# Mish as one ScalarE function, and the layer norm's root by Newton steps on VectorE

## The chip, the cores and the metric

The kernel runs on one core of a Trainium2 chip. Its time is the device time of one execution in microseconds; the time before is the median of three runs. The engines are called as the profile calls them: PE is TensorE (matmuls), ACT is ScalarE, DVE is VectorE, POOL is GpSimd, and SP issues the DMAs.

## What is computed

The reference normalizes `x` (2048 rows of 512) and adds three things: `x` itself, a spectral filter of the normalized rows, and an MLP of them with the Mish activation. Everything is float32.

```python
xn = (x - mean) / sqrt(var + 1e-5)                     # x: (1, 2048, 512)
A  = irfft2(rfft2(xn) * (w_r + 1j * w_i))              # w_r, w_i: (2048, 257)
h  = xn @ w1 + b1                                      # w1: (512, 1792)
sp = log1p(exp(-abs(h))) + where(h > 0, h, 0)          # softplus
B  = (h * tanh(sp)) @ w2                               # w2: (1792, 512)
out = x + A + B
```

## The kernel before

**Precision.** Every float32 operand of a matmul is split into a high and a low float16 part, and each product is three matmuls (`mm3`, lines 64, 67 and 68: high by high, high by low, low by high). A split (`split`, lines 200 and 201) is one pass of ScalarE, which scales and writes the high part, and one of VectorE, which writes the remainder. Before a split, operands are scaled by powers of two that the kernel derives on the chip: of w1 from sums of squares (`load_w1`, `pow2_norm`), of w2 and of the spectral weights from maxima (`w2_scale`, `prep_spectral`). The last step of each is a reduction over the partitions on GpSimd (`qs`, `qa`, and `am` at line 308).

**The MLP.** The 2048 rows are four groups `g` of 512, and the 1792 hidden columns are 14 tiles `f` of 128, so there are 56 tiles. For each tile, `mlp_up` makes `ph` (128 hidden columns by 512 rows) in PSUM by 12 matmuls of 512 columns. Then come six passes for the activation (lines 535 to 543) and the split into `a` (two float16 parts). `mlp_down` makes 12 matmuls that add the tile to four accumulators `pa` in PSUM. It follows `mlp_up` by `LAG` = 2 tiles. `ph` has two PSUM buffers (pool `ps_h`, shared with the transposes `pt`), `hb` and `a` have three each. When a group is done, `mlp_end` adds `x` and writes `m` (line 572), which frees the accumulators.

The activation works on `hb`, which is `h` in units of a power of two. It uses tanh(softplus(h)) = 1 - 2/(n + 2) with n + 2 = (e + 1)^2 + 1 and e = exp(h): a capped copy (VectorE, line 537), exp, square, ln and exp (ScalarE, lines 538 to 542), and the product (VectorE, line 543). The sign is undone by the scale of the split, `s_act`.

**The norm.** `norm(g, ...)` takes statistics of four slices of 128 rows (lines 120 and 122), then the reciprocal root of the variance `ve` for all four at once: ln and exp on ScalarE (lines 126 and 128) and one Newton step on VectorE (lines 131 to 135). `rs` is the result times 1024. Each slice is then normalized (`xs`, line 144), split (`xh`, line 152 on ScalarE, line 153 on GpSimd, in group 0 on VectorE), transposed on TensorE (`pt`, line 157), and copied to `xnT` (lines 158 and 159).

**The transform.** The 2048 by 512 transform is a series of small matmuls: `psS` (first step, `s1_forward`), then for each of four chunks `c` the units `psP`, the spectrum (`ere`, `eim`, `ore`, `oim`, with products on VectorE and GpSimd and the split `u`), `psA`, `psT`, and last `psY` (`s1_inverse`). Between the steps the data goes through DRAM (`d_y1`, `d_a`, `d_t`).

**The order.** All loads are issued by SP. The body is written as one sequence in which the MLP's half tiles are placed between the other work: `b(n)` issues `n` tiles, and `stream_a` is interleaved by counts (`B_END`, `N_UNITS`). The framework then orders each engine's instructions itself, by its own estimate of when they can start; `issue_after` and `keep_in_program_order` tie a few of them. On the chip each engine works through its list strictly in order, so an instruction that waits holds up all that stand behind it.

Of the kernel before, what the change touches and what calls it, by code (L numbers as in the profile page):

```python
# [11 lines left out]
F16 = mybir.dt.float16  # L12
F32 = mybir.dt.float32
# [6 lines left out]
P = 128  # L20
# [9 lines left out]
# column offsets of the packed small constants (fp16 columns)  # L30
# [5 lines left out]
def spectral_mlp_kernel(ctx, tc, x, wt, w0, w1, b1, w2, cT, cIT, cM, out):  # L36
# [14 lines left out]
    nc.scalar.preload_act_table_set("natural_log_exp_and_others")  # L51
# [3 lines left out]
    half = cp.tile([P, 1], F32, tag="half", name="half")  # L55
    nc.gpsimd.memset(half, 0.5)

    d_y1 = dp.tile([64, P, 256], F16, tag="d_y1", name="d_y1")  # [(s2 d2)][(c f1)][hl d1]
    d_a = dp.tile([16, P, 4 * 256], F16, tag="d_a", name="d_a")  # [f1g][(k2p cc j)][f1l hl d1]
    d_t = dp.tile([64, P, 256], F16, tag="d_t", name="d_t")  # [(s2 d2)][(c f1)][hl d1]  # L60

    def mm3(ps, stat, mov, start, stop, order=False):
        """stat(h), mov(h): operands by part; ps += hi*hi + hi*lo + lo*hi"""
        first = nc.tensor.matmul(ps, stat(0), mov(0), start=start, stop=False)  # L64
# [3 lines left out]
        nc.tensor.matmul(ps, stat(1), mov(0), start=False, stop=stop)  # L68

# [45 lines left out]

    def norm(g, ts):
# [8 lines left out]
        lv = sp.tile([P, 4], F32, tag="lv", name=f"lv_{g}", bufs=2)  # L125
        nc.scalar.activation(lv, ve, AF.Ln)
        rr = sp.tile([P, 4], F32, tag="rr", name=f"rr_{g}", bufs=2)
        nc.scalar.activation(rr, lv, AF.Exp, scale=-0.5)
        # a newton step: r <- r * (1.5 - 0.5 v r^2), the result times 2^10
        q1 = sp.tile([P, 4], F32, tag="q1", name=f"q1_{g}", bufs=2)  # L130
        nc.vector.tensor_mul(q1, rr, rr)
        nc.vector.tensor_mul(q1, q1, ve)
# [32 lines left out]
    def pow2_of(name, am, n=1, out_tag=None):  # L165
        """largest powers of two at or below am (at least 2^-60)"""
# [14 lines left out]
    def pow2_norm(name, q, n):  # L181
        """q: n sums of squares per partition; power of two p with sqrt(the whole sum) < 2p"""
# [7 lines left out]
        # halve the exponent: the bits are multiples of 2^23  # L190
# [26 lines left out]
    def load_w1(k):  # L217
        """part k of w1: loaded, and its scale"""
# [21 lines left out]
        # h of these columns comes in units of 2^24/p1  # L240
        s_b = scalars(f"b_{k}", w1sc[k], 1024.0)
        f2 = slice(2 * a, 2 * b)
        nc.vector.tensor_scalar(bs[:, f2], b1t[:, f2], s_b, None, op0=ALU.mult)
        s_cap[k] = scalars(f"cap_{k}", s_b, 9.5)
# [7 lines left out]
    def act_scale():  # L252
        # |h| <= |xn| |w1 column| + |b1| with |xn| < 23
# [5 lines left out]
        s_a = scalars("a", pH, 2.0**14, recip=True)  # L259
        for k in range(2):  # L260
            t = cp.tile([P, 1], F32, tag=f"s_act{k}", name=f"s_act_{k}")
            nc.vector.scalar_tensor_tensor(t, s_a, -1.0, s_exp[k], op0=ALU.mult, op1=ALU.mult)
            s_act[k] = t
# [28 lines left out]
    def prep_spectral():  # L292
# [6 lines left out]
        # chunk c at partitions 32c + f1g: [+re,-re,+im,-im][r][j f1l]  # L299
# [12 lines left out]
        # coefficient tables of slot 0: A' = c0 A + c1 B, B' = c2 A + c3 B  # L312
# [47 lines left out]
    def spectrum(c):  # L360
# [50 lines left out]
        X = tp.tile([P, 4, 256], F32, tag="X", name=f"X_{c}", bufs=2)  # pr, mr, pi, mi  # L411
# [29 lines left out]
        if c == 0:  # L441
            # f = 0 (A) and f = 1024 (B): real sequences with their own weights
# [49 lines left out]
            # partitions (cc j f1l)  # L492
# [27 lines left out]
    macc, yacc = {}, {}  # L520

    def mlp_up(g, f):
        """a tile of hidden columns, and its activation split in two parts"""
# [11 lines left out]
        nc.scalar.activation(hb, ph, AF.Identity, bias=bs[:, f : f + 1])  # L535
        e = mp.tile([P, 512], F32, tag="e", name=f"e_{g}_{f}", bufs=3)
        nc.vector.tensor_scalar(e, hb, s_cap[k], None, op0=ALU.min)  # L537
        nc.scalar.activation(e, e, AF.Exp, scale=s_exp[k])  # L538
        # tanh(softplus(h)) = 1 - 2/(n + 2) with n = e^2 + 2e = (e + 1)^2 - 1
        nc.scalar.activation(e, e, AF.Square, bias=1.0)  # L540
        nc.scalar.activation(e, e, AF.Ln, scale=0.5, bias=half)  # L541
        nc.scalar.activation(e, e, AF.Exp, scale=-1.0)  # L542
        nc.vector.scalar_tensor_tensor(hb, e, 1.0, hb, op0=ALU.subtract, op1=ALU.mult)  # L543
        a = mp.tile([P, 2, 512], F16, tag="a", name=f"a_{g}_{f}", bufs=3)
        split(a[:, 0, :], a[:, 1, :], hb, s_act[k])
# [16 lines left out]
    def mlp_end(g):  # L562
        # the group's transposed rows are done with: x + MLP takes their place
# [12 lines left out]
    def mlp_all():  # L576
        """the MLP, half a tile of hidden columns at a time"""
# [51 lines left out]
    def b(n):  # L629
        """n tiles up, and those down that go with them"""  # L630
# [5 lines left out]
    def stream_a():  # L636
        todo = []  # P2' units, each some way behind its D' unit
# [75 lines left out]
    # the last step of the transform: the last group before its MLP ends, the others as fillers  # L713
# [175 lines left out]
```

## Time and profile before

| | |
|---|---|
| device time, median of 3 runs | 440.85 us (438.7 to 442.54) |
| span of the profiled execution, first to last instruction | 440.4 us |
| difference between the median and that span | 0.45 us |
| TensorE busy | 395.2 us (90%), 2099 matmuls |
| ScalarE busy | 308.5 us (70%), 493 instructions |
| VectorE busy | 301.3 us (68%), 545 instructions |
| GpSimd busy | 44.1 us (10%), 46 instructions |
| share of the 16 DMA engines' span in use by the main queue | 43.2% |
| mean granted TensorE clock | 0.982 of full speed |

The profile is of one execution, whose own device time is not listed apart from the runs; its span is the nearest measure of it. Busy matmuls are pipelined, so a matmul counts for longer than the distance to the next one. In a list of waits, "A <- B" means that engine and line A was idle until B was done. A row of the timeline has the start, the duration, the engine, the line, what is written and read, and in brackets how long the engine was idle just before and what ended that.

### The profile page before, as it was taken

The numbers are of one execution on the slowest core, as the hardware profiler recorded it, in microseconds if no ns is written. First come the engines' busy times: TensorE is split into PE (matmuls) and PEld (weight loads), VectorE is DVE, ScalarE is ACT, GpSimd is POOL, SyncE is SP. The second block draws the span as 40 slices with busy tenths as digits, with TensorE's granted clock in tenths as the row PEclk, the third lists the DMA queues.
The fourth block names the chain that finished last, engine by engine and source line by source line (L and its number), as shares of the span: only waits on it lengthen the run. The fifth ranks groups of instructions, "written<-read, shape, count | busy, mean of one in ns | idle before, by whom it ended". The sixth has DMA issues, their size and how long they took to land. (4 is left out here: it accounts for less than half of the span.)

```text
span 440.4 us, 5858 instructions
## 1 busy us (share of the span) xinstructions
PE 395.2 (90%) x2099; PEld 193.2 (44%) x2099; DVE 301.3 (68%) x545; ACT 308.5 (70%) x493; POOL 44.1 (10%) x46
## 2 busy tenths in 40 slices
PE   0785899699797999989999999999989998899995
PEld 0332344344343445435554445544455544454442
DVE  4969999888557335895569875578855598444564
ACT  2999998867768778468764868756786657576640
POOL 0000003232040000220002020020200022000000
PEclk9998999899899999999999999999999999899999
DMA  8998754487232721032246013342024210233786
GB/s 245 282 360 287 246 188 138 127 262 262 91 101 90 212 80 49 1 89 71 81 142 216 25 48 115 103 133 83 2 71 148 93 50 0 70 122 104 224 292 239
DMA packets 48813, 61.04 MB, mean 139 GB/s; under 512 B 3168, under 2 KB 31360, under 8 KB 48528
## 3 DMA queue, kind: packets, MB, share of 16 engines
q1 hardware_dynamic: 48784, 60.67, 43.2%
q8 instruction: 16, 0.26, 0.2%
q14 instruction: 13, 0.11, 0.1%
HBM read 43.85 MB, written 16.78 MB: 138 GB/s over the span
## 5 line engine op out<-in xcount | busy, mean ns | idle before, releaser
L64 PE MATMUL ph<-xnT,w1t 128*128 128x512 f16 x224 | 85.4, 381 | 5.4 <-ACT hb L535 4.4
L68 PE MATMUL ph<-xnT,w1t 128*128 128x512 f16 x224 | 85.4, 382 | 3.6 <-DVE w1t L201 3.6
L64 PE MATMUL pa<-w2t,a 128*128 128x512 f16 x224 | 85.3, 383 | 2.4 <-DVE m L572 2.4
L68 PE MATMUL pa<-w2t,a 128*128 128x512 f16 x224 | 86.2, 385 | 0.0
L67 PE MATMUL pa<-w2t,a 128*128 128x512 f16 x224 | 86.0, 384 | 0.0
L67 PE MATMUL ph<-xnT,w1t 128*128 128x512 f16 x224 | 85.4, 381 | 0.0
L543 DVE SCALAR_TENSOR_TENSOR hb<-e,hb 128x512 f32<-128x512 f32 x56 | 42.5, 759 | 56.0 <-ACT e L542 55.4
L200 ACT ACTIVATE a<-hb,s_act 128x512 f16<-128x512 f32 x56 | 40.3, 720 | 28.7 <-DVE hb L543 28.7
L538 ACT ACTIVATE e<-e,sc_exp 128x512 f32<-128x512 f32 x56 | 40.2, 719 | 28.1 <-DVE e L537 27.9
L535 ACT ACTIVATE hb<-ph,bs 128x512 f32<-128x512 f32 x56 | 37.9, 677 | 27.4 <-PE ph L68 27.0
L201 DVE SCALAR_TENSOR_TENSOR a<-hb,s_act,a 128x512 f16<-128x512 f32 x56 | 45.6, 813 | 16.6 <-ACT a L200 16.5
L541 ACT ACTIVATE e<-e,half 128x512 f32<-128x512 f32 x56 | 40.4, 721 | 1.6
L537 DVE TENSOR_SCALAR e<-hb,sc_cap 128x512 f32<-128x512 f32 x56 | 28.0, 500 | 16.2 <-ACT hb L535 16.1
L542 ACT ACTIVATE e<-e 128x512 f32<-128x512 f32 x56 | 35.2, 628 | 1.4
L540 ACT ACTIVATE e<-e 128x512 f32<-128x512 f32 x56 | 35.1, 627 | 1.2
L68 PEld LDWEIGHTS <-w1t 128*128 128x128 f16 x224 | 22.0, 98 | 31.1 <-DVE w1t L201 4.5
L67 PEld LDWEIGHTS <-w1t 128*128 128x128 f16 x224 | 22.0, 98 | 30.5 <-issue 6.3
L67 PEld LDWEIGHTS <-a 128*128 128x128 f16 x224 | 22.2, 99 | 27.2 <-issue 4.0
L68 PEld LDWEIGHTS <-a 128*128 128x128 f16 x224 | 22.1, 99 | 26.9 <-issue 1.0
L64 PEld LDWEIGHTS <-w1t 128*128 128x128 f16 x224 | 22.0, 98 | 26.7 <-ACT w1t L200 1.6
L64 PEld LDWEIGHTS <-a 128*128 128x128 f16 x224 | 22.1, 99 | 24.3 <-issue 0.9
L157 PE MATMUL pt<-cMt,xh 128*128 128x128 f16 x128 | 11.6, 244 | 18.7 <-ACT xh L152 11.5
(162 smaller groups left out, 608.5 us busy)
## 6 DMA issues: line engine op xcount, KB each, us to landing
x<-in_x_dram SPq DMA_DIRECT2D x8, 512.0 KB
d_y<-y SPq DMA_DIRECT2D x8, 512.0 KB
wm<-in_wt_dram SPq DMA_DIRECT2D x8, 512.0 KB
yt<-d_y SPq DMA_DIRECT2D x16, 256.0 KB
d_a<-at SPq DMA_DIRECT2D x16, 256.0 KB
ai<-d_a SPq DMA_DIRECT2D x16, 256.0 KB
d_t<-tt SPq DMA_DIRECT2D x16, 256.0 KB
yi<-d_t SPq DMA_DIRECT2D x16, 256.0 KB
```

Of the source, the lines that this page charges most:

```text
L64: first = nc.tensor.matmul(ps, stat(0), mov(0), start=start, stop=False)
L67: nc.tensor.matmul(ps, stat(0), mov(1), start=False, stop=False)
L68: nc.tensor.matmul(ps, stat(1), mov(0), start=False, stop=stop)
L200: hi = nc.scalar.activation(dst_h, src, AF.Copy, scale=scale)
L201: nc.vector.scalar_tensor_tensor(dst_l, src, scale, dst_h, op0=ALU.mult, op1=ALU.subtract)
L535: nc.scalar.activation(hb, ph, AF.Identity, bias=bs[:, f : f + 1])
L537: nc.vector.tensor_scalar(e, hb, s_cap[k], None, op0=ALU.min)
L538: nc.scalar.activation(e, e, AF.Exp, scale=s_exp[k])
L540: nc.scalar.activation(e, e, AF.Square, bias=1.0)
L541: nc.scalar.activation(e, e, AF.Ln, scale=0.5, bias=half)
L542: nc.scalar.activation(e, e, AF.Exp, scale=-1.0)
L543: nc.vector.scalar_tensor_tensor(hb, e, 1.0, hb, op0=ALU.subtract, op1=ALU.mult)
```

## The change

**The activation.** `mlp_up` now has one ScalarE pass, the function Mish, which reads `ph` from PSUM, multiplies by `s_exp` (so that `h` comes in its own units) and adds the bias `b1`. The tiles `e`, the caps `s_cap`, the scaled bias `bs`, the constant `half` and the negative scales `s_act` are gone. The split into `a` stays, with the scale `sc["a"]`. Of the six passes for each tile one is left: ScalarE has two passes for each tile in place of six (with the split), and VectorE one in place of three.

**The root.** `rsqrt_of` takes a first value from the bits of `ve` by one integer operation, and makes three Newton steps of three VectorE instructions each; the last instruction multiplies by -128, which makes up for the constants left out of the steps. That is eleven instructions on VectorE in place of two on ScalarE and four on VectorE, each on 128 by 4 values.

**The table.** The function table that ScalarE loads at the start is now the one with Mish, in place of the one with ln and exp. The program has one table load, as before.

```diff
-    nc.scalar.preload_act_table_set("natural_log_exp_and_others")
+    nc.scalar.preload_act_table_set("mish")
...
+    def rsqrt_of(g, ve):
+        r = sp.tile([P, 4], F32, tag="rr", name=f"rr_{g}_0", bufs=4)
+        nc.vector.tensor_scalar(
+            r.bitcast(I32), ve.bitcast(I32), -0.5, float(0x5F3759DF), op0=ALU.mult, op1=ALU.add
+        )
+        for k in range(3):
+            t = sp.tile([P, 4], F32, tag="rt", name=f"rt_{g}_{k}", bufs=2)
+            nc.vector.tensor_mul(t, r, r)
+            q = sp.tile([P, 4], F32, tag="rq", name=f"rq_{g}_{k}", bufs=2)
+            nc.vector.scalar_tensor_tensor(q, t, 0.25**k, ve, op0=ALU.mult, op1=ALU.mult)
+            n = sp.tile([P, 4], F32, tag="rr", name=f"rr_{g}_{k + 1}", bufs=4)
+            nc.vector.scalar_tensor_tensor(n, q, 3.0, r, op0=ALU.subtract, op1=ALU.mult)
+            r = n
+        rs = sp.tile([P, 4], F32, tag="rs", name=f"rs_{g}", bufs=2)
+        nc.vector.tensor_scalar(rs, r, -128.0, None, op0=ALU.mult)
+        return rs
...
-        nc.scalar.activation(lv, ve, AF.Ln)
-        nc.scalar.activation(rr, lv, AF.Exp, scale=-0.5)
-        nc.vector.tensor_mul(q1, rr, rr)
-        nc.vector.tensor_mul(q1, q1, ve)
-        nc.vector.tensor_scalar(q1, q1, -512.0, 1536.0, op0=ALU.mult, op1=ALU.add)
-        nc.vector.tensor_mul(rs, rr, q1)
+        rs = rsqrt_of(g, ve)
...
-        nc.scalar.activation(hb, ph, AF.Identity, bias=bs[:, f : f + 1])
-        nc.vector.tensor_scalar(e, hb, s_cap[k], None, op0=ALU.min)
-        nc.scalar.activation(e, e, AF.Exp, scale=s_exp[k])
-        nc.scalar.activation(e, e, AF.Square, bias=1.0)
-        nc.scalar.activation(e, e, AF.Ln, scale=0.5, bias=half)
-        nc.scalar.activation(e, e, AF.Exp, scale=-1.0)
-        nc.vector.scalar_tensor_tensor(hb, e, 1.0, hb, op0=ALU.subtract, op1=ALU.mult)
+        nc.scalar.activation(hb, ph, AF.Mish, bias=b1t[:, f : f + 1], scale=s_exp[k])
         a = mp.tile([P, 2, 512], F16, tag="a", name=f"a_{g}_{f}", bufs=3)
-        split(a[:, 0, :], a[:, 1, :], hb, s_act[k])
+        split(a[:, 0, :], a[:, 1, :], hb, sc["a"])
```

With other instructions in the program the framework's order changes too. Three places matter below. Lines of the new kernel are some 10 lower than those of the old for the same statement.

**TensorE, the first product with w2.** In the names, `ph_0_6` is group 0, tile 6, and `pa_0_0` is the first of group 0's four accumulators. Before:

```order
L64 MATMUL ph_0_6_559<-xnT_0_124,w1t_92 128x512
L64 LDWEIGHTS a_0_0_294
L64 MATMUL pa_0_0_416<-w2t_93,a_0_0_294 128x512
L64 LDWEIGHTS a_0_0_294
L64 MATMUL pa_0_1_417<-w2t_93,a_0_0_294 128x512
```

Now:

```order
L64 MATMUL ph_0_7_551<-xnT_0_133,w1t_90 128x512
L65 LDWEIGHTS w1t_90
L65 MATMUL ph_0_7_551<-xnT_0_133,w1t_90 128x512
L61 LDWEIGHTS a_0_0_282
L61 MATMUL pa_0_0_390<-w2t_91,a_0_0_282 128x512
```

Before, seven of the twelve matmuls of tile 6 stood ahead of the first `pa`; now all of tiles 6 and 7 do, 17 matmuls more. Behind this point the order of TensorE's work is nearly the same in both.

**VectorE, the root of norm 1.** `xs_4` is the first normalized slice of group 1, `st_2` and `st_3` are statistics of groups 2 and 3, and `a_0_7` is a split. Before:

```order
L131 TENSOR_TENSOR q1_1_736<-rr_1_734 128x4
L120 BN_STATS st_2_997<-x_2_0_992 128x6
L201 SCALAR_TENSOR_TENSOR a_0_6_581<-hb_0_6_572,s_act_1_270,a_0_6_581 128x512
L132 TENSOR_TENSOR q1_1_736<-q1_1_736,ve_1_730 128x4
L120 BN_STATS st_2_997<-x_2_0_992 128x6
L133 TENSOR_SCALAR q1_1_736<-q1_1_736 128x4
L120 BN_STATS st_2_997<-x_2_1_994 128x6
L135 TENSOR_TENSOR rs_1_740<-rr_1_734,q1_1_736 128x4
L120 BN_STATS st_2_997<-x_2_1_994 128x6
L543 SCALAR_TENSOR_TENSOR hb_0_7_618<-e_0_7_620,hb_0_7_618 128x512
L144 TENSOR_SCALAR xs_4_743<-x_1_0_600,mv_1_721,rs_1_740 128x512
```

Now (the chain has begun 12 rows ahead of these):

```order
L139 BN_AGGR mv_2_907<-st_2_906 128x2 x2
L127 SCALAR_TENSOR_TENSOR rr_1_2_669<-rq_1_1_667,rr_1_1_663 128x4
L137 BN_STATS st_3_1145<-x_3_0_1140 128x6
L123 TENSOR_TENSOR rt_1_2_671<-rr_1_2_669 128x4
L141 TENSOR_SCALAR ve_2_916<-mv_2_907 128x4
L137 BN_STATS st_3_1145<-x_3_0_1140 128x6
L125 SCALAR_TENSOR_TENSOR rq_1_2_673<-rt_1_2_671,ve_1_655 128x4
L127 SCALAR_TENSOR_TENSOR rr_1_3_675<-rq_1_2_673,rr_1_2_669 128x4
L117 TENSOR_SCALAR rr_2_0_918<-ve_2_916 128x4
L130 TENSOR_SCALAR rs_1_677<-rr_1_3_675 128x4
L123 TENSOR_TENSOR rt_2_0_920<-rr_2_0_918 128x4
L151 TENSOR_SCALAR xs_4_680<-x_1_0_546,mv_1_646,rs_1_677 128x512
```

The longer chain has more statistics between its steps, those of `x_3_0` among them, which is loaded after `x_2`.

**VectorE, the scale of the spectral weights.** `cl_W` reads `am`, GpSimd's reduction; `xnT_2` are the copies that free the buffers of group 2's transposes, and `y1_8` frees a buffer of the first transform step. Before:

```order
L158 COPY xnT_2_1019<-pt_8_1025 128x4x128
L543 SCALAR_TENSOR_TENSOR hb_0_13_967<-e_0_13_969,hb_0_13_967 128x512
L158 COPY xnT_2_1019<-pt_9_1048 128x4x128
L106 SCALAR_TENSOR_TENSOR y1_8_1040<-psS1_8_1036,y1_8_1040 128x4x128
L201 SCALAR_TENSOR_TENSOR a_0_13_976<-hb_0_13_967,s_act_1_270,a_0_13_976 128x512
L158 COPY xnT_2_1019<-pt_10_1071 128x4x128
L106 SCALAR_TENSOR_TENSOR y1_8_1040<-psS1_9_1059,y1_8_1040 128x4x128
L158 COPY xnT_2_1019<-pt_11_1094 128x4x128
L168 TENSOR_SCALAR cl_W_1546<-am_1544 128x1
```

Now:

```order
L208 SCALAR_TENSOR_TENSOR a_0_13_885<-hb_0_13_883,sc_a_264,a_0_13_885 128x512
L175 TENSOR_SCALAR cl_W_1430<-am_1428 128x1
L177 TENSOR_SCALAR p2_W_1432<-cl_W_1430 128x1
L165 COPY xnT_2_940<-pt_8_946 128x4x128
L183 RECIPROCAL sc_u_1434<-p2_W_1432 128x1
L185 TENSOR_SCALAR sc_k_1437<-p2_W_1432 128x1
L185 TENSOR_SCALAR sc_u_1434<-sc_u_1434 128x1
L165 COPY xnT_2_940<-pt_9_969 128x4x128
```

The wait for `am` stood behind all four copies of group 2 and now stands ahead of the first.

More of the change, by code (lines that the diff above doesn't have):

```diff
@@ L49, in spectral_mlp_kernel @@
     dp = ctx.enter_context(tc.tile_pool(name="dp", bufs=1, space=bass.MemoryType.DRAM))
-    nc.scalar.preload_act_table_set("natural_log_exp_and_others")
+    nc.scalar.preload_act_table_set("mish")
     xv = x.rearrange("(p s) d -> p s d", s=NS2)
     outv = out.rearrange("(p s) d -> p s d", s=NS2)
-    half = cp.tile([P, 1], F32, tag="half", name="half")
-    nc.gpsimd.memset(half, 0.5)
     d_y1 = dp.tile([64, P, 256], F16, tag="d_y1", name="d_y1")
@@ L124, in norm @@
         nc.vector.tensor_scalar(ve, mv[:, :, 1], 1e-5, None, op0=ALU.add)
-        lv = sp.tile([P, 4], F32, tag="lv", name=f"lv_{g}", bufs=2)
-        nc.scalar.activation(lv, ve, AF.Ln)
[L127 to L132, printed above, removed]
-        nc.vector.tensor_scalar(q1, q1, -512.0, 1536.0, op0=ALU.mult, op1=ALU.add)
-        rs = sp.tile([P, 4], F32, tag="rs", name=f"rs_{g}", bufs=2)
-        nc.vector.tensor_mul(rs, rr, q1)
+        rs = rsqrt_of(g, ve)
         xT = cp.tile([P, 2, 4, 512], F16, tag=f"xnT{g}", name=f"xnT_{g}")
@@ L207, in spectral_mlp_kernel @@
     b1t = cp.tile([P, NFC], F32, tag="b1", name="b1t")
-    bs = cp.tile([P, NFC], F32, tag="bs", name="bs")
-    s_cap, s_exp, s_act = {}, {}, {}
+    s_exp = {}
     sc = {}
@@ L239, in load_w1 @@
         w1sc[k] = scalars(f"w1_{k}", p1, 2.0**14, recip=True)
[L241 to L244, printed above, removed]
         s_exp[k] = scalars(f"exp_{k}", p1, 2.0**-24)
@@ L258, in act_scale @@
         pH = pow2_of("H", hb_)
[L259 to L263, printed above, removed]
+        sc["a"] = scalars("a", pH, 2.0**14, recip=True)
         sc["pH"] = pH
@@ L534, in mlp_up @@
         hb = mp.tile([P, 512], F32, tag="hb", name=f"hb_{g}_{f}", bufs=3)
[L535 to L543, printed above, removed]
+        nc.scalar.activation(hb, ph, AF.Mish, bias=b1t[:, f : f + 1], scale=s_exp[k])
         a = mp.tile([P, 2, 512], F16, tag="a", name=f"a_{g}_{f}", bufs=3)
-        split(a[:, 0, :], a[:, 1, :], hb, s_act[k])
+        split(a[:, 0, :], a[:, 1, :], hb, sc["a"])
         return a
```

## Prediction

> **What bounds the kernel now.** I read the page first for the engine that is fullest, then the busy time by stage, then the waits of that engine.
>
> ```profile
> PE 395.2 (90%) x2099; PEld 193.2 (44%) x2099; DVE 301.3 (68%) x545; ACT 308.5 (70%) x493; POOL 44.1 (10%) x46
> PE   0785899699797999989999999999989998899995
> PEclk9998999899899999999999999999999999899999
> ```
>
> TensorE (PE) is busy for 395.2 of 440.4 us. ScalarE (ACT) and VectorE (DVE), from which the change takes work, are busy for only 70 and 68%. So removed work does not count by its own length; it counts where TensorE waits for it, at most 440.4 - 395.2 = 45.2 us and what a lowered clock costs. The next view has the engines' busy time by stage (columns: stretch, length, then busy us and count for each engine, granted clock, DMA share, GB/s).
>
> ```profile
> 0.00:48.00 48.00, 26.69 (x126) 11.82 (x127) 35.78 (x90) 37.73 (x61) 2.25 (x9) 0.96 0.89 289
> 48.00:76.00 28.00, 28.00 (x131) 12.73 (x130) 27.35 (x51) 25.36 (x40) 2.81 (x2) 1.00 0.59 191
> 76.00:141.00 65.00, 55.08 (x306) 26.93 (x304) 48.40 (x91) 48.88 (x86) 15.60 (x19) 0.95 0.49 155
> 141.00:381.00 240.00, 231.33 (x1282) 116.58 (x1279) 159.28 (x271) 168.13 (x267) 23.42 (x16) 0.99 0.27 85
> 381.00:441.00 60.00, 54.09 (x264) 25.14 (x261) 30.50 (x46) 28.35 (x44) 0.00 (x0) 0.98 0.58 189
> ```
>
> TensorE's idle time is 21.3 us in the first stage (loading, first norm, w1 and w2 scales), 0 in the second, 9.9 in the third (norms 1 to 3 between MLP tiles), 8.7 in the fourth (transform and MLP together) and 5.9 at the end. The second stage gives the price of a large matmul that waits for nothing: 28.00 / 131 = 0.214 us. The granted clock is a loss that is no idle time. The page's clock line has an 8 in four of its slices of 11 us (the 4th, 8th, 11th and 35th); the stage means say what one costs: 0.95 over 65 us is 3.3 us lost for two of them, 0.96 over 48 us 1.9 for one. I use 1.7 for each. Whom TensorE waited for (us in total, times, longest):
>
> ```profile
> PE pt L157 <- ACT xh L152: 11.5, 1, 11.5
> PE pt L157 <- ACT xnT L159: 7.1, 3, 3.6
> PE ph L64 <- ACT hb L535: 4.4, 3, 1.7
> PE ph L68 <- DVE w1t L201: 3.6, 2, 3.3
> PE psA L64 <- ACT u L200: 3.1, 4, 1.6
> PE pa L64 <- DVE m L572: 2.4, 3, 1.3
> PE oim L64 <- DVE w L452: 2.1, 1, 2.1
> PE psA L68 <- DVE u L201: 1.9, 4, 0.7
> ```
>
> None of these is the wait for an activated tile `a`: the activation itself is hidden by the two tiles of lag. All are waits for other work in the queues of ScalarE and VectorE, behind which the six passes stand.
>
> **The activation, by its price.** The removed and kept passes, from the page (count | busy, mean ns of one):
>
> ```profile
> L543 DVE SCALAR_TENSOR_TENSOR hb<-e,hb 128x512 f32<-128x512 f32 x56 | 42.5, 759 | 56.0 <-ACT e L542 55.4
> L538 ACT ACTIVATE e<-e,sc_exp 128x512 f32<-128x512 f32 x56 | 40.2, 719 | 28.1 <-DVE e L537 27.9
> L535 ACT ACTIVATE hb<-ph,bs 128x512 f32<-128x512 f32 x56 | 37.9, 677 | 27.4 <-PE ph L68 27.0
> L541 ACT ACTIVATE e<-e,half 128x512 f32<-128x512 f32 x56 | 40.4, 721 | 1.6
> L537 DVE TENSOR_SCALAR e<-hb,sc_cap 128x512 f32<-128x512 f32 x56 | 28.0, 500 | 16.2 <-ACT hb L535 16.1
> L542 ACT ACTIVATE e<-e 128x512 f32<-128x512 f32 x56 | 35.2, 628 | 1.4
> L540 ACT ACTIVATE e<-e 128x512 f32<-128x512 f32 x56 | 35.1, 627 | 1.2
> ```
>
> ScalarE loses 40.2 + 35.1 + 40.4 + 35.2 = 150.9 us and falls to about 158; VectorE loses 42.5 + 28.0 = 70.5. The new pass takes the place of L535 with one more per-partition operand. The trace has no Mish, so I bound it: 0.677 us (L535, also from PSUM) below, and above 2.7 us, as if it cost the four removed passes together. I take 0.72, the row with a scale operand; either end keeps ScalarE below TensorE's 5.1 us for a tile (24 x 0.214), so the ends change the sum by no more than the range below.
>
> **The root, by its price.** Rows of the first norm: two steps of the old chain, the first pass on VectorE that uses it, and ScalarE's square of w1 ahead of the cast that the transposes wait for.
>
> ```profile
> 8.18 0.16 DVE L131 TENSOR_TENSOR q<-rr 128x4 f32<-128x4 f32 x1 [0.51 <-ACT rr L128]
> 8.38 0.16 DVE L132 TENSOR_TENSOR q<-q,ve 128x4 f32<-128x4 f32 x1
> 8.98 1.00 DVE L144 TENSOR_SCALAR xs<-x,mv,rs 128x512 f32<-128x512 f32 x2
> 9.76 1.06 ACT L230 ACTIVATE w1t<-w1s 128x1024 f16<-128x1024 f32 x1 [1.61 <-DMA w1s<-in_w_dram]
> ```
>
> A dependent step is 0.20 us. Eleven steps after 7.68 (end of `ve`) end near 9.9, so `xs` starts about 0.9 later than 8.98. The cast stands behind the square, which ends at 10.82 because its DMA came late; `xs` is there by 10.4. I cost this at nothing; without that cover it would be 0.9 us. In the later norms the steps are interleaved: before the first `xs` of norm 1 the new queue has the statistics of x_3_0, a load later than in the old one, and norm 2's first steps. GpSimd, which makes the low parts, sets the pace of those norms anyway.
>
> **First stage: 3 us gained.** TensorE now does 17 more `ph` matmuls before the first `pa`: 17 x 0.214 = 3.6 us of work done while it waits for w2's scale. That scale does not come sooner: three w1 splits that stood behind it on VectorE now stand ahead, and take the time that the cap and product passes leave. The longest hole stays, as the four w2 reductions still precede the w1 split:
>
> ```profile
> 35.94 0.61 PE L68 MATMUL ph<-xnT,w1t 128*128 128x512 f16 x1 [3.27 <-DVE w1t L201]
> ```
>
> So 3.0, with bounds of 0 (the scale is late by what was won) and 6 (two of the three `hb` waits go too).
>
> **Third stage: 6.6 us gained.** The two long waits of the transposes, and what surrounds them:
>
> ```profile
> 80.71 1.21 DVE L297 TENSOR_REDUCE mxw<-wm 128x1 f32<-128x1024 f32 x1
> 82.53 0.57 ACT L159 COPY xnT<-pt 128x512 f16<-128x512 f16 x1
> 83.14 0.92 PE L157 MATMUL pt<-cMt,xh 128*128 128x128 f16 x8 [3.58 <-ACT xnT L159]
> 112.85 0.61 PE L157 MATMUL pt<-cMt,xh 128*128 128x128 f16 x8 [2.78 <-ACT xnT L159]
> 116.03 0.38 POOL L308 PARTITION_ALL_REDUCE am<-mxwa  x1 [9.28 <-DVE y L106]
> 124.23 2.26 POOL L153 TENSOR_TENSOR xh<-xs,xh 128x512 f16<-128x512 f32 x2 [7.82 <-ACT e L541]
> ```
>
> The first wait (3.58) I keep whole: ScalarE's copy comes sooner, but VectorE's copy still stands behind the wm reduction and now behind norm 2's and 3's steps. The second (2.78) loses ScalarE's four passes, but in the new VectorE queue the scale that needs `am` moves ahead of the first transposed copy. GpSimd idles 9.28 us before that all-reduce and 7.82 after it, beside an extra unnamed row of its own in the program, and I take both to stay. The reductions ahead of it come some 9 us sooner, since their queue waits less for ScalarE, so I put `am` at about 107 (116.4 before) and TensorE there at 106: 1.0 of the wait is left, 1.8 goes, and the slow clock behind it, 1.7. The `m` waits (2.4) and the last transposes' 0.7 (7.1 - 3.6 - 2.8) go with the passes among them. 1.8 + 1.7 + 2.4 + 0.7 = 6.6; bounds -5 (`am` no sooner than before: TensorE would wait 10.4 there in place of 2.8, less the other 3.1) and 13 (9.9 + 3.3).
>
> That clock is the place for one rule: the waits of 3.58 and 2.78 end in the 8th and 11th slice, which show the lower clock, and the 2.1 of `oim`, near 191 us in the 18th, shows none. [...]
>
> **Fourth stage: 7.5 us gained.** Behind `oim` stands a serial chain of VectorE, GpSimd, ScalarE, VectorE to `psA`:
>
> ```profile
> 369.78 0.68 DVE L469 TENSOR_TENSOR o<-oim,wO 128x512 f32<-128x512 f32 x1
> 370.60 1.76 DVE L543 SCALAR_TENSOR_TENSOR hb<-e,hb 128x512 f32<-128x512 f32 x1
> 372.28 0.68 DVE L470 TENSOR_TENSOR o<-oim,wO 128x512 f32<-128x512 f32 x1
> ```
>
> The removed L543 sits inside it for 1.76 us, with others ahead. Of the 5.0 us of `psA` waits I leave 1.0, of 2.1 for `oim` 1.0 (it also moves up by 8 matmuls on TensorE), and take 0.7 from the 1.6 that are left of the stage's 8.7: 4.0 + 1.1 + 0.7, and 1.7 of slow clock in the 35th slice, just behind the chain shown. Bounds 3 (one long `psA` wait and its clock) and 10.4 (8.7 + 1.7).
>
> **The end: 0.5.** TensorE's last matmul is the bound there:
>
> ```profile
> 435.52 0.38 PE L68 MATMUL pa<-w2t,a 128*128 128x512 f16 x1
> ```
>
> The chain of waits runs through the last tile's six passes, but TensorE has inverse-transform and `pa` work under them until 435.5. What follows stays.
>
> **The sum.** 3.0 + 6.6 + 7.5 + 0.5 = 17.6: 440.4 - 17.6 = 422.8 for a profiled span. The median of the runs, 440.85, lies 0.45 above the span: **423 us**.
>
> **Rivals.**
> *Nearly all waits go.* TensorE keeps only the start and the tail: the sum by the upper bounds is 6 + 13 + 10.4 + 1 = 30.4, so 410. For it: ScalarE at 158 us has room everywhere. Against it: VectorE's queue is in order and full of waits for loads. Chance 0.15 (under 415).
> *The holes stay where loads and GpSimd make them.* Stage three gives 0 and stage one 1: 440.85 - 9 = 432, or 436 with half of stage four. For it: the 9.28 and 7.82 us of GpSimd, and the DMA share of 0.89 in the first stage. Chance 0.19.
> *Slower, by `am`.* The place is VectorE's queue at the second transposes, now closed until `am` comes. Each us that `am` is later than 107 costs one, and a long wait costs 1.7 of clock: from 107 + 17.6 - 1.7 = 123 on the kernel is slower than before, and at 130 it takes 448. The longer root chain and the statistics ahead of it can delay `am`; against it stands that before, with all passes in the queue, it came at 116.4. Chance 0.04.
> *The one function isn't one.* If Mish shared no table with copy and square, each tile would switch tables twice:
>
> ```profile
> 0.72 1.28 ACT L51 ACT_TABLE_LOAD   x1 [0.72 <-PEq L862]
> ```
>
> 112 x 1.28 = 143 us would give back what ScalarE won (150.9), and the time would be about 440. Against it: the new program has one table load, as the old. Chance 0.02. [...]
>
> **How the numbers follow.** The forecast (415 to 431) has the remaining 0.60. A change within 1% can't be told from none here; 1% of 440.85 puts the limits at 436.4 and 445.3. The table case and 0.03 of the second rival fall between, 0.03 of the third above: 0.92, 0.05, 0.03. The range runs from the first rival's 410 to 434, inside the second's.
>
> **What would show it.** Right: ScalarE near 158 busy, VectorE near 235, one Mish row of 0.68 to 0.75 us; waits of `psA` under 1.5 in sum; the first `pa` still near 47, with 8 `ph` tiles done; a wait of `pt` near 80 still there, with a slow clock behind it. Wrong: `am` after 112, a wait of TensorE for `a`, or the first `pa` after 50.

## The result, and the profile after

The changed kernel takes **425.75 us** (median of 4 runs, 424.21 to 427.87); the kernel before took 440.12 beside it (median of 4, 438.70 to 442.54). The ratio is 0.969 with a 95% interval of 0.964 to 0.975. The profiled execution has a span of 424.4 us. In a later series of runs the same program gave 424.39 (0.968, 0.964 to 0.971). The forecast was 423, with 410 to 434 as its range.

The page of the changed kernel, busy time and the two lines that were shown of before:

```profile
PE 391.0 (92%) x2099; PEld 194.1 (46%) x2099; DVE 241.3 (57%) x453; ACT 172.4 (41%) x261; POOL 42.2 (10%) x45
PE   0787899499899999989999999999999999999995
PEclk9999999889999999989999999999999999999999
```

ScalarE gave up 136 us of busy time and VectorE 60; the kernel got 16 us shorter in its span. TensorE is busy 4.2 us less and idle 11.8 us less (33.4 for 45.2). Where the idle time went is read from the stages (columns as before: stretch, length, busy us and count of PE, PEld, DVE, ACT, POOL, granted clock, DMA share, GB/s; the last stretch reaches past the span by 0.6):

```profile
0.00:48.00 48.00, 29.32 (x142) 13.72 (x143) 34.95 (x83) 30.24 (x45) 2.75 (x8) 1.00 0.90 294
48.00:76.00 28.00, 27.24 (x136) 12.52 (x134) 26.69 (x61) 15.40 (x21) 4.39 (x4) 1.00 0.60 187
76.00:141.00 65.00, 57.99 (x317) 28.49 (x314) 41.73 (x77) 29.13 (x49) 13.27 (x18) 0.95 0.57 178
141.00:381.00 240.00, 237.87 (x1334) 122.27 (x1333) 119.81 (x208) 90.43 (x138) 21.75 (x16) 0.99 0.27 86
381.00:425.00 44.00, 38.59 (x178) 17.10 (x176) 18.12 (x26) 7.20 (x10) 0.00 (x0) 0.98 0.66 215
```

TensorE's idle time by stage is now 18.7, 0.8, 7.0, 2.1 and 4.8 us (21.3, 0, 9.9, 8.7 and 5.3 before, the last one without the 0.6 us past the span). The fourth stage gave most. The third gave 2.9 us of idle time and nothing of slow clock, where 6.6 us were foretold with both. Whom TensorE waits for (us in total, times, longest):

```profile
PE pt L164 <- ACT xh L159: 11.3, 1, 11.3
PE pt L164 <- ACT xnT L166: 6.6, 2, 5.6
PE ph L65 <- DVE w1t L208: 2.4, 2, 2.1
PE oim L61 <- DVE w L450: 2.1, 1, 2.1
PE pa L61 <- ACT w2t L207: 1.6, 1, 1.6
```

`psA` and `m` have left the list, and no row names `a`. One wait has grown: the transposes' 3.6 us near 80 us is now 5.6. The new pass, by the page:

```profile
L533 ACT ACTIVATE hb<-ph,b1t,sc_exp 128x512 f32<-128x512 f32 x56 | 43.4, 775 | 107.4 <-PE ph L65 104.2
```

Mish costs 0.775 us for 128x512 from PSUM. ScalarE now stands idle for 107.4 us ahead of it, nearly all of that for the matmul that feeds it.

### The profile page after: what moved, and what is told of

It reads as the page before. It is cut to its first block, busy times and chain, and to the rows that moved or that the text cites. A ratio compares the mean times of both kernels' runs of the same rounds, so it can differ in the third digit from the quotient of the medians.

```text
span 424.4 us, 5542 instructions
## 1 busy us (share of the span) xinstructions
PE 391.0 (92%) x2099; PEld 194.1 (46%) x2099; DVE 241.3 (57%) x453; ACT 172.4 (41%) x261; POOL 42.2 (10%) x45
## 4 chain that ended last, share of the span: by engine, by line
PE 72%; DVE 13%; DMA 6%; ACT 4%; issue 2%; POOL 0%; SPq 0%; DVEq 0%; ACTq 0%; POOLq 0%
PE pa L65 9%; PE pa L64 9%; PE pa L61 9%; PE ph L61 9%; PE ph L65 9%; PE ph L64 9%; DVE q L273 2%; DMA w1s<-in_w_dram 2%; PE pt L164 2%; ACT w1t L236 1%; PE psA L61 1%; PE psA L64 1%; PE psA L65 1%; DMA w2s<-in_w_dram 1%; DMA ai<-d_a 1%
## 5 line engine op out<-in xcount | busy, mean ns | idle before, releaser
L533 ACT ACTIVATE hb<-ph,b1t,sc_exp 128x512 f32<-128x512 f32 x56 | 43.4, 775 | 107.4 <-PE ph L65 104.2
L208 DVE SCALAR_TENSOR_TENSOR a<-hb,sc_a,a 128x512 f16<-128x512 f32 x56 | 42.3, 755 | 76.2 <-ACT a L207 76.1
L207 ACT ACTIVATE a<-hb,sc_a 128x512 f16<-128x512 f32 x56 | 40.1, 719 | 2.2 <-PE pa L65 0.9
L65 PEld LDWEIGHTS <-w1t 128*128 128x128 f16 x224 | 21.9, 98 | 29.7 <-DVE w1t L208 3.4
L64 PEld LDWEIGHTS <-w1t 128*128 128x128 f16 x224 | 21.9, 98 | 27.1 <-issue 2.3
L61 PEld LDWEIGHTS <-w1t 128*128 128x128 f16 x224 | 21.9, 98 | 26.4 <-ACT w1t L207 1.6
L164 PE MATMUL pt<-cMt,xh 128*128 128x128 f16 x128 | 12.3, 253 | 18.5 <-ACT xh L159 11.3
L487 DVE SCALAR_TENSOR_TENSOR at<-psA,at 128x512 f16<-128x512 f32 x16 | 11.0, 689 | 19.1 <-ACT at L486 19.1
L422 POOL TENSOR_TENSOR w<-X,wE 128x512 f32<-128x512 f32 x4 | 5.1, 1269 | 165.7 <-ACT er L387 76.8
L164 PEld LDWEIGHTS <-xh 128*128 128x128 f16 x128 | 10.3, 114 | 23.7 <-ACT xh L159 12.0
L509 DVE SCALAR_TENSOR_TENSOR tt<-psT,tt 128x512 f16<-128x512 f32 x16 | 11.0, 690 | 14.1 <-ACT tt L508 13.9
L160 POOL TENSOR_TENSOR xh<-xs,xh 128x512 f16<-128x512 f32 x12 | 14.4, 1216 | 45.2 <-ACT xh L159 29.9
L486 ACT ACTIVATE at<-psA 128x512 f16<-128x512 f32 x16 | 9.4, 589 | 22.8 <-PE psA L65 22.8
```

Of the source, the lines that this page charges most:

```text
L160: (nc.vector if g == 0 else nc.gpsimd).tensor_sub(xh[:, 1, :], xs, xh[:, 0, :])
L164: nc.tensor.transpose(pt[:, h, dc, :], xh[:, h, dc * P : (dc + 1) * P], ident)
L207: hi = nc.scalar.activation(dst_h, src, AF.Copy, scale=scale)
L208: nc.vector.scalar_tensor_tensor(dst_l, src, scale, dst_h, op0=ALU.mult, op1=ALU.subtract)
L486: nc.scalar.mul(at[:, :, 0, :], ps, 2.0**-15)
L487: nc.vector.scalar_tensor_tensor(at[:, :, 1, :], ps, 2.0**-15, at[:, :, 0, :], op0=ALU.mult, op1=ALU.subtract)
```

## The experiments

All times are medians beside runs of the kernel before on the same chip; the ratio is to those runs. The rows come from several series on different chips, and the kernel before had medians from 439.02 to 441.03 in them; so two rows are compared by their ratios too, and 2 us between two medians show nothing by themselves. "Idle" is TensorE's, from the same five stretches of each profile (length less busy time; the last one up to the span's end).

| kernel | us | ratio, 95% interval | idle 0-48 | 48-76 | 76-141 | 141-381 | rest | clock |
|---|---|---|---|---|---|---|---|---|
| before | 440.12 | 1 | 21.3 | 0 | 9.9 | 8.7 | 5.3 | 0.982 |
| changed | 425.75 | 0.969 (0.964-0.975) | 18.7 | 0.8 | 7.0 | 2.1 | 4.8 | 0.986 |
| changed, again | 424.39 | 0.968 (0.964-0.971) | 18.5 | 1.0 | 7.5 | 2.2 | 5.1 | 0.985 |
| root alone | 442.12 | 1.003 (1.000-1.006) | 20.2 | 0 | 10.1 | 8.4 | 5.8 | 0.978 |
| short root | 421.38 | 0.954 (0.950-0.958) | 15.8 | 0 | 3.3 | 2.5 | 4.4 | 0.978 |
| VectorE's passes back | 431.50 | 0.977 (0.974-0.981) | 19.3 | 0.3 | 10.1 | 2.6 | 4.6 | 0.983 |
| ScalarE's passes back | 427.09 | 0.966 (0.962-0.970) | 20.3 | 0 | 5.6 | 2.4 | 5.3 | 0.984 |
| both back | 438.47 | 0.996 (0.992-0.999) | 19.8 | 1.2 | 9.4 | 6.5 | 5.6 | 0.979 |
| two steps | 422.70 | 0.958 (0.953-0.964) | 18.4 | 0.3 | 7.0 | 2.2 | 5.0 | 0.994 |
| copies on ScalarE | 423.13 | 0.962 (0.954-0.969) | 17.3 | 1.0 | 6.5 | 2.2 | 4.7 | 0.988 |
| copies and two steps | 422.38 | 0.959 (0.953-0.965) | 17.1 | 0.3 | 6.3 | 2.3 | 4.8 | 0.986 |
| copies, two steps, held behind norm 2 | 432.99 | 0.988 (0.984-0.992) | 17.1 | 0.3 | 11.1 | 7.0 | 5.1 | 0.980 |
| first root short | 424.35 | 0.969 (0.965-0.973) | 15.9 | 0 | 5.8 | 2.2 | 4.8 | 0.978 |
| copies, two steps, held behind norm 1 | **418.17** | 0.951 (0.948-0.954) | 17.3 | 0.4 | 2.6 | 2.4 | 4.4 | 0.989 |

The order within each engine is chosen by the framework, so every edit also shifts some neighbours; the stages above show where.

### The two halves of the change apart

**The root alone**, with the old six passes:

```
 kernel before:
-  lv = Ln(ve); rr = Exp(-0.5 lv)          # ScalarE
-  one Newton step                          # VectorE
+  rs = rsqrt_of(g, ve)                     # 11 VectorE operations
```

> The kernel before with the layer norm's root by Newton steps on VectorE, and all six activation passes and their table kept. Theory (the gain is the activation's alone, the root is hidden): no change, 438 to 442 us beside 440.1, first wait of pt still 11.5 us, the pt wait near 80 us between 3.5 and 5. Rival (the longer chain on VectorE delays the transposes and is paid for out of the activation's gain): 443 to 447 us, with pt waits 3 us or more longer in sum than the 18.6 of before.

442.12 us, 0.3% slower with an interval that reaches to no change: the gain of the change is the activation's. The `m` waits rose from 2.4 to 3.3 us. The pt waits did not grow in sum (17.3 us for 18.6), but the one near 80 us went from 3.6 to 4.5.

**The activation with a short root**:

```
 def rsqrt_of(g, ve):
-  for k in range(3):
+  for k in range(0):
-  rs = r * -128.0
+  rs = r * 1024.0
```

> The changed kernel with the root's three Newton steps left out (two VectorE operations of 128x4 per norm are left, so the rows are normalised by a root that is off by up to some per cent). Theory (the root is hidden): 424.5 to 427 us, as the changed kernel's 425.75. Rival (nine steps per norm, some of them of 1.1 us beside GpSimd, are in the 5.6 us wait of the transposes near 82 us and perhaps in the 11.3 us of the first): 420 to 424 us, the wait near 82 us under 4.5 us.

421.38 us, in the rival's range and 3.0 to 4.4 us below the two medians of the changed kernel (by the ratios to before, some 6). So the root, costed at nothing, costs 3 to 6 us in the new kernel, with what the framework reorders around it. Its longest waits:

```profile
PE pt L164 <- ACT xh L159: 9.1, 1, 9.1
PE pa L61 <- ACT w2t L207: 4.3, 1, 4.3
PE pt L164 <- ACT xnT L166: 2.8, 1, 2.8
```

Both pt waits are shorter: the first by 2.2 us, the one near 80 by 2.8. Which of them pays? The next kernel shortens the **first norm's root alone**:

```
-  for k in range(3):
+  for k in range(3 if g else 0):
-  rs = r * -128.0
+  rs = r * (-128.0 if g else 1024.0)
```

> The changed kernel with the Newton steps left out in the first norm alone (whose rows are then normalised by a root that is off by up to some per cent); norms 1 to 3 keep all three steps. If what the root costs lies at the start (the cast gets ahead of w1's square on ScalarE and the transposes start 2 us sooner): 421 to 423.5 us. If it lies in norms 2 and 3 (the steps in the queue near 80 us): 424.5 to 426 us, with the 5.6 us wait still there.

424.35 us, beside 424.39 for the changed kernel in the same series: nothing. The transposes do start 2.2 us sooner, and the first `pa` 2.0 us sooner, at 45.69. But that one now waits 4.3 us for w2 in place of 1.6, and three half-clock periods come in the first two stages, where the changed kernel has none. So TensorE gets to the wait near 80 us at 76.6, as against 77.0: the lead is nearly gone. That wait is still 5.0 us long:

```profile
PE pt L164 <- ACT xnT L166: 5.0, 1, 5.0
```

By difference, the price of the root lies in norms 1 to 3. Idle time points to the third stage (3.3 us with the short root everywhere, 5.8 with it in the first norm alone), and there to the wait near 80 us (2.8 and 5.0). No run shortened the later roots alone.

> The changed kernel itself, as it is, beside the other two on one chip, to compare with: 424 to 427 us if its 425.75 holds, and the half-clock periods at about the same places.

This was the control of that series. Its lowered clock stands at the same places as in the first profile.

### Which engine's passes mattered

The kernels here put the removed load back into every tile, between Mish and the split, without changing a value.

```
 hb = Mish(ph)
+e = min(hb, 1e30)                  # VectorE's passes back
+hb = max(e * 1.0, hb)
```

> The changed kernel with two VectorE passes put back into every tile between Mish and the split, which change no value: a minimum with 1e30 (0.50 us in the trace of before) and a product and maximum (0.76 us). VectorE is then as full as before (about 305 us), ScalarE as empty as after (172). Theory (it was VectorE's queue that held psA): 431 to 435 us, psA waits of 3 us or more in sum are back. Rival (it was ScalarE's queue): 424 to 428 us and psA waits under 1.5 us.

```
 hb = Mish(ph)
+e = copy(hb); e = copy(e), three times; hb = e   # ScalarE's passes back
```

> The changed kernel with four ScalarE copies put back into every tile between Mish and the split, which change no value. ScalarE is then as full as before (about 315 us), VectorE as empty as after (241). Theory (VectorE's queue held psA, ScalarE's four passes cost only the waits for hb and the last transposes): 427 to 430 us, psA waits under 1.5 us. Rival (ScalarE's queue): 431 to 436 us, with psA waits of 3 us or more and longer waits for hb and xnT.

```
 hb = Mish(ph)
+four ScalarE copies, then the two VectorE passes  # both back
```

> The changed kernel with four ScalarE copies and then two VectorE passes put back into every tile between Mish and the split; they change no value. Both engines are as full as before, but a tile goes back and forth between them twice (ScalarE, VectorE, ScalarE, VectorE) and not three times. Theory (load: it takes both engines full for psA to wait, as neither alone brought it back): 437 to 441 us, psA waits of 3 us or more. Rival (the crossings: a tile that goes from queue to queue more often is what held psA): about the sum of the two single runs, 425.75 + 5.75 + 1.3 = 432.8, so 431 to 435 us, psA under 1.5 us.

The third and fourth stage of the three profiles, in that order of kernels (VectorE's, ScalarE's, both):

```profile
76.00:141.00 65.00, 54.87 (x307) 27.20 (x306) 53.15 (x102) 29.98 (x51) 18.06 (x21) 0.95 0.56 167
141.00:381.00 240.00, 237.38 (x1326) 121.45 (x1325) 154.07 (x274) 88.75 (x136) 21.75 (x16) 0.99 0.29 88
```

```profile
76.00:141.00 65.00, 59.37 (x326) 29.00 (x325) 38.43 (x70) 49.89 (x84) 12.04 (x17) 0.92 0.54 165
141.00:381.00 240.00, 237.65 (x1340) 122.44 (x1339) 122.86 (x208) 170.47 (x276) 22.22 (x16) 1.00 0.28 88
```

```profile
76.00:141.00 65.00, 55.62 (x300) 26.67 (x299) 53.36 (x100) 47.71 (x82) 19.08 (x21) 0.92 0.52 163
141.00:381.00 240.00, 233.54 (x1303) 119.19 (x1303) 158.47 (x274) 163.95 (x268) 22.84 (x16) 0.99 0.28 86
```

The times first: VectorE's passes cost 5.75 us against 425.75 (3.6 by the ratios), both together 12.7 (11.6), most of the gain. ScalarE's alone cost 1.3, or by the ratios gain 1.2, which is no difference that can be told from none. The two stages behave differently. In the third, the idle time goes by VectorE alone: 10.1 us with its passes, 5.6 with ScalarE's, 7.0 with neither; ScalarE's bring one more half-clock period there (0.92 for 0.95). In the fourth, neither alone matters (2.6 and 2.4 beside 2.1), and both together bring back 4.4 of the 6.6 us. So my expectation that VectorE's queue held `psA` was wrong: with its passes back the time came into the range foreseen for that, but by the third stage, and the psA waits were 0.4 us, not 3. The `psA` wait with VectorE's passes back, and then the `psA` and `psT` waits with both:

```profile
PE psA L65 <- DVE u L208: 0.4, 1, 0.4
```

```profile
PE psA L65 <- DVE u L208: 2.0, 2, 1.6
PE psT L61 <- DVE at L487: 1.3, 1, 1.3
PE psA L61 <- DVE at L487: 1.1, 2, 0.6
```

The rival of the last run, that the number of crossings between the engines did it, falls too: here a tile crosses less often than in the kernel before, and psA waits 3.1 us again (5.0 before). 2.0 of these are for `u`, at the end of the chain behind `oim`, which goes through both engines' queues; the other 1.1 are for VectorE's `at`. That one engine with room shortens the chain enough is my reading of the three runs; no run takes the chain apart.

### The wait near 80 us

VectorE, ScalarE and GpSimd of the changed kernel around it (start, length, engine, line, operation, idle before; rows left out are marked by dots):

```profile
71.02 1.08 DVE L125 SCALAR_TENSOR_TENSOR rq<-rt,ve 128x4 f32<-128x4 f32 x1
...
74.26 1.13 DVE L130 TENSOR_SCALAR rs<-rr 128x4 f32<-128x4 f32 x1
...
75.50 1.26 DVE L151 TENSOR_SCALAR xs<-x,mv,rs 128x512 f32<-128x512 f32 x1
...
77.81 0.68 DVE L137 BATCH_NORM_STATS2 st<-x 128x6 f32<-128x512 f32 x1
...
79.62 1.21 DVE L295 TENSOR_REDUCE mxw<-wm 128x1 f32<-128x1024 f32 x1
80.75 0.74 DVE L208 SCALAR_TENSOR_TENSOR a<-hb,sc_a,a 128x512 f16<-128x512 f32 x1
...
81.48 0.42 DVE L165 COPY xnT<-pt 128x512 f16<-128x512 f16 x1
```

```profile
81.93 0.58 ACT L166 COPY xnT<-pt 128x512 f16<-128x512 f16 x1 [5.50 <-DVE xnT L165]
82.41 0.60 ACT L102 ACTIVATE y<-psS 128x512 f16<-128x512 f32 x1
82.90 0.62 ACT L159 CAST xh<-xs 128x512 f16<-128x512 f32 x1
```

```profile
69.81 2.27 POOL L160 TENSOR_TENSOR xh<-xs,xh 128x512 f16<-128x512 f32 x2 [25.22 <-ACT xh L159]
73.89 2.60 POOL L160 TENSOR_TENSOR xh<-xs,xh 128x512 f16<-128x512 f32 x2 [1.80 <-ACT xh L159]
```

TensorE started its last matmul ahead of the wait at 76.61 and the next transposes at 82.57, when the copies had emptied `pt`. VectorE reached its half of the copy at 81.48, behind the root's steps, norm 3's statistics and a wm reduction (one of the eight maxima of the spectral weights); ScalarE stood idle for 5.50 us, since its half waits for VectorE's (in all 16 pairs of this profile it starts after VectorE's has ended, by 0.03 to 1.35 us). Three small operations (0.16 us elsewhere) took 1.08, 1.13 and 1.16 while GpSimd's subtraction ran. Two edits attack this place:

```
 for k, c in ((0, 3.0018), (1, 3.0000015)):      # two steps
     t = r * r
     q = t * (0.25**k * 2**-16) * ve
     r = (q - c) * r                             # no closing product
```

> The changed kernel with two Newton steps in place of three, with their constants set for it (worst relative error of the root about 8e-7), and the closing multiplication folded into the seed: 7 small VectorE operations per norm after the variance in place of 11. Theory (each small operation costs, in proportion): 11 operations gave 425.75 and 2 gave 421.4, so 0.48 us each and 423.8 here, 423 to 424.6 us. Rival (thresholds: what counts is whether the first cast gets ahead of the square of w1 on ScalarE, and whether the steps fall ahead of the transposed copy near 80 us): either as with 2 operations, 421 to 422 us, or as with 11, 425 to 426.5 us.

```
 if g:                                           # copies on ScalarE
+    nc.scalar.copy(xTv[:, :, :, s, :], pt)
-    nc.vector.tensor_copy(xTv[:, 0, ...], pt[:, 0])
-    nc.scalar.copy(xTv[:, 1, ...], pt[:, 1])
```

> The changed kernel with both halves of the transposed copies of norms 1 to 3 on ScalarE as one copy of 1024 elements; the first norm is left as it is, and so is the root. Theory (the 5.58 us wait near 82 us is VectorE's queue: the wm reduction and the root's steps stand ahead of the copy of the first half, and ScalarE's copy waits for that one): the wait falls under 1.5 us, the slow clock behind it goes or halves, 419 to 423 us. Rival (something else is as late there: GpSimd's low parts or the next rows' xs): the wait is still over 3 us with another releaser, 424 to 427 us.

> Both of the last two edits together. If they remove different waits (the root's cost at the start of the kernel, the copies' near 82 us): 417 to 420.5 us. If both only shorten the same wait near 82 us: 420.5 to 423 us, as the better of the two alone.

Two steps gave 422.70, between the ranges of the two expectations, and it settles nothing: its wait near 80 us is 5.6 as before, its idle time 0.5 us less than the changed kernel's, and the rest of the profiled difference is two half-clock periods that did not come (0.994 for 0.986). The copies gave 423.13, and the wait stayed, as the rival said, though for neither of the reasons that it named.

```profile
83.06 0.58 PE L61 MATMUL psS<-xh,cTt 128*128 128x512 f16 x1 [5.62 <-DVE y L103]
```

TensorE now waits for `psS`, which VectorE's `y` empties from the same place in the same queue. Both edits together gave 422.38, as each alone. What is late is VectorE's queue, not one reader of it. So the next edit, on top of both, holds back what stands ahead:

```
+last_y = norm(2, load_x(2))                     # "held behind norm 2"
+with tc.issue_after(last_y):                    # in VectorE's queue
     norm(3, xs3)
 ...
+    with tc.issue_after(last_y):
         nc.vector.tensor_reduce(mxw[:, c], wm_c)
```

> The kernel with the copies on ScalarE and the two-step root, and in VectorE's queue norm 3's operations and the eight wm reductions are held behind norm 2's last y, the operation that empties psS. Theory (the wait of 5.6 to 6 us near 80 us only moved, from the copy to y, as both stand behind the same reductions and statistics in VectorE's queue): it falls under 1.5 us here and the slow clock behind it goes, 414 to 418 us. Rival (the reductions then push the spectral scale am past norm 3): the time is 419 us or more, with a wait of pt or psS after 100 us of over 3 us.

432.99 us, as the rival said: the wait near 80 is gone from the list, and the third stage has more idle time (11.1 us) than in the kernel before (9.9). TensorE's longest wait, and GpSimd's rows, which show why:

```profile
PE pt L160 <- POOL xh L156: 13.1, 2, 12.5
```

```profile
137.20 0.38 POOL L307 PARTITION_ALL_REDUCE am<-mxwa  x1 [6.03 <-issue]
144.66 2.26 POOL L156 TENSOR_TENSOR xh<-xs,xh 128x512 f16<-128x512 f32 x2 [7.08 <-issue]
```

The scale came at 137 instead of 110, and the last two slices of norm 3 got their low parts behind it; TensorE waited 12.5 us for them, with three half-clock periods in a row. Held behind **norm 1's** last `y` instead (one name changed, 25 us earlier in the queue):

> As the run that held norm 3's operations and the wm reductions behind norm 2's last y, but they are held behind norm 1's last y, some 25 us sooner in VectorE's queue. In that run the wait near 80 us was gone and a wait of 12.5 us for GpSimd's low parts, behind the spectral scale's all-reduce, had come after 130 us. Theory (both waits follow from where the reductions stand in VectorE's queue): neither is there now; from the 422.4 us of the two edits alone go the wait of 5.9 us and 2 to 3.4 us of slow clock: 413 to 417 us, and it is the fastest kernel here. Rival (the scale comes late here too, by the 5 us that the statistics and reductions are held up): 419 to 424 us, with a wait of pt for GpSimd's low parts of over 3 us between 105 and 125 us.

418.17 us, the fastest kernel here, 4.9% below before (ratio 0.951, 0.948 to 0.954). Its longest waits:

```profile
PE pt L160 <- ACT xh L155: 11.0, 1, 11.0
PE ph L65 <- DVE w1t L207: 2.4, 2, 2.1
PE oim L61 <- DVE w L450: 2.0, 1, 2.0
PE pa L61 <- DVE m L562: 1.6, 1, 1.6
```

Idle time in the third stage is 2.6 us of 65, with a granted clock of 1.00. The scale comes as in the changed kernel; GpSimd in the one here, and then in the changed kernel:

```profile
109.06 0.38 POOL L306 PARTITION_ALL_REDUCE am<-mxwa  x1 [7.42 <-issue]
116.18 2.26 POOL L156 TENSOR_TENSOR xh<-xs,xh 128x512 f16<-128x512 f32 x2 [6.74 <-issue]
```

```profile
109.91 0.38 POOL L306 PARTITION_ALL_REDUCE am<-mxwa  x1 [7.99 <-PE psS L65]
117.36 2.27 POOL L160 TENSOR_TENSOR xh<-xs,xh 128x512 f16<-128x512 f32 x2 [7.08 <-issue]
```

The median is 1 us above the expected 413 to 417; no wait of pt for low parts is in the list, so the theory's two waits are both gone. The order of one queue at one place was worth 4.2 us beside the kernel with the two edits alone (3.4 by the ratios), where the whole change is worth 14.4.

## Why the prediction was right, and where its steps were not

- **The bound.** Right: removed passes counted only where TensorE waited. 221 us of passes went, and 14.4 us of time.
- **The activation's price.** Mish is 0.775 us, above my 0.72 and the foretold row of 0.68 to 0.75. ScalarE ended at 172, not 158. Of these 14 us, 5.5 are Mish (43.4 for L535's 37.9). Most of the rest is that I subtracted summed durations from busy time that overlaps: back to back, its operations start 0.48 us apart and last 0.58 or 0.60 (the rows at 81.93 and 82.41), and the durations of all its operations sum to 20.9 us more than its busy time before, and to 10.6 more now. VectorE's 241 for 235 has the same overlap in it (29.0 us before, 21.9 now), and the root's 44 operations took 10.1 us where 0.16 each would be 7.0, as four of them ran beside GpSimd's subtraction and took 1.16, 1.13, 1.08 and 0.41. None of this reached the time: with ScalarE back at 302 us the kernel took 427.09, no clear difference.
- **The root at nothing.** This step failed. At the start it held (the wait is 11.3 for 11.5, and even a start 2.2 us sooner gave nothing). In the later norms I left it to GpSimd's pace, and the short root showed 3 to 6 us, by difference none of it at the start: idle time in the third stage is 3.3 us with it and 7.0 without.
- **First stage, 3.0.** Idle time fell by 2.6, and the slow clock of 1.7 us there went too. The mechanism held: 96 `ph` matmuls ran before the first `pa`, 79 before, and that one came at 47.66. Which waits went was not foretold as it came: two for `hb` (1.71 and 1.65) are gone and one of 1.59 for w2 is new. The hole behind the w1 split, which I had kept, shrank from 3.27 to 2.1. The second stage gave back 0.8.
- **Third stage, 6.6.** Measured 2.9 of idle time and no less slow clock (0.95 in both): the term that was most wrong. The second pt wait went as foretold (2.78 to 0.98, its slow clock with it), the `m` waits too, and the scale came at 110.3, where GpSimd's reduction ends, with TensorE there at 110.7 (forecast 107 and 106). But the first wait, "kept whole", grew by 2.0: TensorE was there 2.6 us sooner (77.0 for 79.6), VectorE's copy only 0.4 (81.48 for 81.84). So most of what the first stage had gained was lost again here, and the slow clock behind the wait doubled. The gains of stages add up only if the next wait moves too: I let TensorE come sooner, left the end of this wait where VectorE's queue put it, and still kept its length.
- **Fourth stage, 7.5.** Measured 6.6 of idle time. The size held, the cause did not: I named VectorE's pass inside the chain, and its return alone brought nothing back. `psA` went to no wait at all (1.0 left in my sum), `oim` stayed at 2.1 (1.0). The slow clock behind `psA` went, but one came behind `oim`, so the 1.7 of clock was not won; with two steps the same wait had none behind it, so this was chance (last section).
- **The end, 0.5.** 0.5.

The idle terms give 2.6 - 0.8 + 2.9 + 6.6 + 0.5 = 11.8; TensorE's busy time fell by 4.2, of which one half-clock period less is 1.7. Of the other 2.5, some 0.7 are short waits: a large matmul's row is 0.38 long at steps of 0.214 to 0.216, so waits of under 0.17 us are counted as busy, and behind large matmuls at full clock the steps of 0.22 to 0.39 exceed 0.216 by 0.86 us in sum before and by 0.12 now. The rest stays open. That the sum came so near was in part luck: too much for the third stage and for the clock in the fourth met terms that I had not counted (the first stage's clock, the busy time).

Of the rivals, the holes at loads and GpSimd was the nearest in its mechanism and too pessimistic in its size; the slower one, by the scale, was built by accident: at 137 us it gave 432.99, some 15 above the kernel that differs by the hold alone. There the scale comes 28 us sooner, so my price of one us for each us would have given 28.

## What to carry to other kernels

When passes are taken from two engines that are not the bound, look for the waits that need both to be full and for those that one queue makes alone. Here the former went whichever engine was relieved (fourth stage: 2.6 and 2.4 us idle with one full, 6.5 with both), and the latter stayed until that queue's order was changed (third stage: 6.3 us idle with the two edits, 2.6 with the hold behind norm 1). Cheap operations of 0.2 us were not free here (the root's cost 3 to 6 us), in a queue ahead of the operation that empties a PSUM tile: look at what stands ahead of that operation, not at its length alone. Before moving a reader to another engine, ask what else is emptied from the same place in the same queue.

## What the runs showed of the hardware

**The lowered clock came in cells of 3.41 us.** In each profile the half-clock periods ahead of the kernel's end are 3.41 us long or a multiple, and their starts lie multiples of 3.41 apart: before, 3.41 each from 35.48, 83.27, 113.99 and 376.82 (14, 9 and 77 cells apart); in the changed kernel, 6.83 from 81.61 and 3.41 from 184.01 (30 cells apart). The same wait for `oim` of 2.05 us, at 180.79 to 182.84 and 178.84 to 180.89, was followed by half clock in the changed kernel and by none with two steps. The cell that holds it and the next one, in TensorE's busy us and granted clock (changed, two steps, and before with its wait of 2.15):

```profile
180.60:184.00 3.40, 1.35 (x7) 1.00 0.13 13
184.00:187.40 3.40, 3.40 (x10) 0.50 0.39 142
```

```profile
177.28:180.69 3.41, 1.56 (x8) 1.00 0.00 0
180.69:184.10 3.41, 3.21 (x15) 1.00 0.50 154
```

```profile
189.10:192.50 3.40, 1.53 (x8) 1.00 0.19 25
192.50:195.90 3.40, 3.40 (x17) 1.00 0.34 130
```

The row of a large matmul (0.38) lasts 0.17 us longer than its step of 0.214 to the next, so by steps these three cells have 2.22, 2.04 and 1.88 us of idle time, and the first alone was followed by half clock. Laid out over the 14 profiles in this way, from the first full clock to 405 us, all 34 full-clock cells with more than 2.2 us idle were followed by a half-clock cell, none of some 1490 with less than 1.9 was, and of the 13 between three were; six of the 34 are in the profiles of before (four) and of the changed kernel (two). So in these profiles a wait of about 2 us cost 1.7 more (half a cell) or nothing, by how much of it fell into one cell. The wait of 5.6 near 80 us was followed by two half-clock cells in the changed kernel, where it reached 0.96 us into the first of them, and by one with two steps, where it reached 0.21 in (third stage: granted clock 0.95 and 0.97).

**Small VectorE operations beside GpSimd.** Operations of 128x4 that take 0.16 us elsewhere took 1.08 and 1.13 in the rows at 71.02 and 74.26, while GpSimd's subtraction of 128x512 ran (69.81 to 72.08, 73.89 to 76.49). The 1.1 was no fixed price: the operation lasted until the subtraction had ended. In the 14 profiles 41 of the norms' 128x4 operations started while one ran; 39 of them ended 0.015 to 0.028 us after it, whether that made them 0.19 or 1.16 us long (in the changed kernel 0.41 to 1.16, before 1.15), and the other two took 0.16. One pass for `xs`, at 75.50, took 1.26 where two take 1.00 in the first norm's row.

**GpSimd around its all-reduce** stood idle for 6.0 to 9.3 us ahead of it and for 6.7 to 7.8 behind it in the four kernels whose rows are shown (before, changed, and the two with the hold).

**A queue held up by one of its instructions.** In the changed kernel the transposes of `pt_8` ended at 108.94. VectorE stood idle for 2.06 us, until `cl_W` had its `am` at 110.32, and their copy, which stands behind `cl_W` in the list, came at 110.58.
